# First norms inside the fourth row tile's statistics, K's second half turned earlier, first scores in two query halves: attention with a fused gated FFN on one core

## The chip, the cores and the metric

The kernel runs on one core of one Trainium2 chip. The metric is the device time of one execution in microseconds (us); lower is better. "Same" means within 2% of the kernel before. Times quoted are medians of fast runs unless one run is named; no run of this study fell into the slow state (a single run of a one-core program has no state of its own and is only used as one look).

Engines are named as the profile names them: PE is TensorE's matmul stream, PEld its weight loads, DVE is VectorE, ACT is ScalarE, POOL is GpSimd, SP is the engine that issues most DMAs. Positions in the trace are microseconds from the start of the span.

## The reference

Layer norm, then attention with 32 heads of width 192 over 2048 cached keys, times a gated FFN on the same normed input, with a residual. Cut to what matters:

```python
x: (1, 2048, 640)   k_cache, v_cache: (1, 32, 2048, 192)   wq: (640, 6144)   wo: (6144, 640)   # bf16
xn = _layernorm(x)
q  = (xn @ wq).reshape(B, Sq, H, Dh)
p  = softmax(einsum("bhqd,bhkd->bhqk", q, k_cache) * Dh ** -0.5)
s  = einsum("bhqk,bhkd->bhqd", p, v_cache).reshape(B, Sq, H * Dh) @ wo
g  = _silu((_silu(xn @ w1) * (xn @ w3)) @ w2)
return x + s * g
```

## The kernel before

The kernel walks a stream of steps `(head, query block, key pair)`. Each step does scores on PE, exponentials on ACT, values on PE. Before the stream there is an opening, `head_start`, that has to produce the first normed and transposed inputs, the first head's turned K, and the first projected queries. Query block 0 is built from four row tiles, in two pairs.

```python
def head_start():
    load_x(0, 0, 2); load_x(0, 2, 4)
    load_k0(0, nc.sync)                       # K of head 0, first half
    load_w0()
    turn_over(44)                             # warming matmuls
    ln_stats(0, 0); ln_stats_act(0, 1)
    load_k0(1, nc.scalar)                     # K of head 0, second half
    # ... more loads
    ln_stats(0, 2)
    # ...
    ln_rstd(0, 1)                             # POOL: inverse deviation of the first pair
    ln_stats(0, 3)                            # ends with POOL's work for the second pair
    load_w(1)
    for i in range(4):
        ln_norm(0, i, nc.vector)
    pk0 = ps_o.tile(...)
    ln_turn(0, 0, nc.scalar.copy)             # PE: transpose the first pair
    turn_k0(pk0, 0, range(4))                 # PE: transpose K, first half
    ln_turn(0, 1, nc.vector.tensor_copy)      # PE: transpose the second pair
    turn_k0(pk1, 1, (0, 1))                   # PE: transpose K, second half, first two slices
    swap_halves(0)                            # two DMAs: xnS = xnT with its partition halves exchanged
    # copies of the turned K, loads
    project_first()
    turn_k0(pk1, 1, (2, 3))
    copy_k0(nc.scalar.copy, pk1, 1, 1)
    scores(0)
    shift_first()                             # DVE: queries moved between partition halves
    shift_k0()                                # DVE: the same for K
    scores(1)
    ln_stats(1, 0); ln_stats(1, 1); ln_stats(1, 2)
    ln_norm(1, 0, nc.vector); ln_norm(1, 1, nc.vector)
    ln_turn_dma(1, 0); ln_turn_dma(1, 1)      # transposed by DMA, not by PE
    # ...
```

```python
def swap_halves(g):
    qs = slice(g * 512, (g + 1) * 512)
    nc.sync.dma_start(out=xnS[0:64, :, qs], in_=xnT[64:P, :, qs])
    nc.sync.dma_start(out=xnS[64:P, :, qs], in_=xnT[0:64, :, qs])

def shift_first():
    qAB, qC = q_tiles(0, 0)
    nc.vector.tensor_copy(out=qC[64:P, 0, :], in_=qAB[0][0:64, :])
    nc.vector.tensor_copy(out=qC[0:64, 0, :], in_=qAB[0][64:P, :])

def two_products(W, qs):                      # a projection as pairs of half-height products
    for j in range(2 * DC):
        for r in range(2):
            xs = xnT if j % 2 == r else xnS   # every second operand is the exchanged copy
            nc.tensor.matmul(ps[:, r * 512:(r + 1) * 512], lhsT=W[rows, j, :], rhs=xs[rows, j // 2, qs], ...)
```

Early in the stream, still during head 0's first query block, two projections follow:

```python
if h == 0 and qb == 0 and p == 3:
    project(1, 0)       # two_products: needs xnS of block 0; its result is cast by DVE and ACT
# ... at p == 3 also: ln_turn(1, 1): PE transposes the second pair of block 1 into the buffer that cast has freed
if h == 0 and qb + 1 < NQB and p == (5 if qb == 0 else 4):
    project0(qb + 1)    # qb == 0: needs all of block 1, half of it transposed by ln_turn_dma
```

Of the kernel before, what the change touches and what calls it, by code (L numbers as in the profile page):

```python
# [12 lines left out]
F32 = mybir.dt.float32  # L13
I32 = mybir.dt.int32

P = 128
# [112 lines left out]
def _kernel_impl(  # L129
# [12 lines left out]
    nc = tc.nc  # L142
# [68 lines left out]
    loads = {}  # L211
# [56 lines left out]
    def turn_k0(dst, half, sel):  # L268
        for a in sel:
            for b in range(HP):  # L270
                nc.tensor.transpose(out=dst[:, a, b * P:(b + 1) * P],  # L271
                                    in_=k0["v"][:, half * HP + b, FIRST[a]:FIRST[a] + P], identity=ident_bf[:])
# [32 lines left out]

    lnorm = {}

    def ln_stats(g, i):
        if i == 0:
            lnorm[g] = [lnp.tile([P, 4, n], F32, tag=t, name=t)  # L310
                        for t, n in (("mv", nc.vector.BN_AGGR_DIM), ("ve", 1), ("rstd", 1))]
        mv, ve, rstd = lnorm[g]
        stats = lnp.tile([P, nsub, nc.vector.BN_STATS_DIM], F32, tag="stats", name="stats")
        xr = x_sb[:, 4 * g + i, :].rearrange("p (a f) -> p a f", a=nsub)
        for a in range(nsub):
            nc.vector.bn_stats(out=stats[:, a, :], in_=xr[:, a, :])  # L316
        nc.vector.bn_aggr(out=mv[:, i, :], in_=stats[:])
        if i % 2 == 1:
            nc.vector.tensor_scalar(out=ve[:, i - 1:i + 1, 0], in0=mv[:, i - 1:i + 1, 1], scalar1=eps, scalar2=None,
                                    op0=ALU.add)  # L320
            ln_rstd(g, i)
# [27 lines left out]
    def ln_turn(g, i2, copy):  # L349
        pst = ps_st.tile([P, 2, DC, P], BF16, tag="st2", name="pst")  # L350
        for k in range(2):
            xn = xns.pop((g, 2 * i2 + k))
            for c in range(DC):
                nc.tensor.transpose(out=pst[:, k, c, :], in_=xn[:, c * P:(c + 1) * P], identity=ident_bf[:])  # L354
        q0 = (4 * g + 2 * i2) * P
        copy(out=xnT[:, :, q0:q0 + 2 * P].rearrange("p c (k q) -> p k c q", k=2), in_=pst[:])
# [11 lines left out]
    qtiles = {}  # L368
# [12 lines left out]
    def project_first():  # L381


        W = loads[0]["W"]
        qAB, qC = q_tiles(0, 0)
        for hh in range(2):
            hs = slice(hh * 256, (hh + 1) * 256)
            ps = ps_st.tile([P, 1024], F32, tag="st2", name="ps0")
            for half in range(2):
                for c in range(DC):  # L390
                    nc.tensor.matmul(ps[:, half * 512:half * 512 + 256], lhsT=W[:, half * DC + c, :], rhs=xnT[:, c, hs],  # L391
                                     start=(c == 0), stop=(c == DC - 1))
            i0 = nc.vector.tensor_copy(out=qAB[0][:, hs], in_=ps[:, 0:256])
            i1 = nc.scalar.copy(out=qAB[1][:, hs], in_=ps[:, 512:768])
            tc.declare_no_dep(i1.ins, i0.ins, reason="two banks, two destinations")
        nc.vector.tensor_copy(out=qC[0:64, 1, :], in_=qAB[1][64:P, :])
# [71 lines left out]

    stream = [(h, qb, p) for h in range(H) for qb in range(NQB) for p in range(NPAIR)]

    def emit_scores(h, qb, p):


        KW = loads[h]["KW"]
        (qA, qB), qC = qtiles[h, qb]
        ks = slice(p * P, (p + 1) * P)
        st2 = ps_st.tile([P, 1024], F32, tag="st2", name="st2")
        rounds = [(KW[0:64, 0, ks], qA[0:64, :], KW[64:P, 1, ks], qC[64:P, 0, :]),
                  (KW[0:64, 3, ks], qC[0:64, 0, :], KW[64:P, 4, ks], qA[64:P, :]),
                  (KW[0:64, 1, ks], qC[0:64, 1, :], KW[64:P, 2, ks], qB[64:P, :])]  # L480
        if (h, qb) == (0, 0) and p < 2:
            rounds = rounds[2:]
            nc.tensor.matmul(st2[:, 0:512], lhsT=KW[:, 0, ks], rhs=qA[:], start=True, stop=False)
            nc.tensor.matmul(st2[:, 512:1024], lhsT=KW[:, 4, ks], rhs=qA[:], start=True, stop=False)
        nr = len(rounds)
        for r, (ka, qa, kb, qb2) in enumerate(rounds):
            nc.tensor.matmul(st2[:, 0:512], lhsT=ka, rhs=qa, start=r == 0 and nr == 3, stop=r == nr - 1)  # L487
            nc.tensor.matmul(st2[:, 512:1024], lhsT=kb, rhs=qb2, start=r == 0 and nr == 3, stop=r == nr - 1)  # L488
        pT2 = pp.tile([P, 1024], BF16, tag="pT2", name="pT2")
        parts = 2 if (h, qb, p) == (0, 0, 0) else 1  # L490
        w = 1024 // parts
        for c in range(parts):
            nc.scalar.activation(out=pT2[:, c * w:(c + 1) * w], in_=st2[:, c * w:(c + 1) * w], func=ACT.Exp, scale=att_scale)  # L493
        return pT2
# [75 lines left out]
    def turn_over(k):  # L570
        for i in range(k):
            nc.tensor.matmul(warm, lhsT=ident_bf[:], rhs=ident_bf[:], start=True, stop=True)

    def head_start():

        load_x(0, 0, 2)
        load_x(0, 2, 4)
        load_k0(0, nc.sync)
        load_w0()
        turn_over(44)  # L580
        ln_stats(0, 0)
        ln_stats_act(0, 1)
        load_k0(1, nc.scalar)
        load_x(1, queue=nc.scalar)
        load_v(0, (0,), nc.scalar)
        mv, ve, _ = lnorm[0]
        nc.vector.tensor_scalar(out=ve[:, 0, :], in0=mv[:, 0, 1:2], scalar1=eps, scalar2=None, op0=ALU.add)
        ln_stats(0, 2)
        nc.vector.tensor_scalar(out=ve[:, 1, :], in0=lnorm["ss"][:], scalar1=1.0 / D, scalar2=eps,
                                op0=ALU.mult, op1=ALU.add)  # L590
        ln_rstd(0, 1)
        ln_stats(0, 3)
        load_w(1)
        for i in range(4):
            ln_norm(0, i, nc.vector)
        pk0 = ps_o.tile([P, 4, 512], BF16, tag="ob0", name="pk0")
        ln_turn(0, 0, nc.scalar.copy)
        turn_k0(pk0, 0, range(4))
        ln_turn(0, 1, nc.vector.tensor_copy)
        turn_k0(pk1, 1, (0, 1))  # L600
        swap_halves(0)
        copy_k0(nc.scalar.copy, pk0, 0, 0)
        copy_k0(nc.scalar.copy, pk0, 0, 1)
        copy_k0(nc.vector.tensor_copy, pk1, 1, 0)
        load_v(0, (1,))
        load_x(2)
        project_first()
        turn_k0(pk1, 1, (2, 3))
        copy_k0(nc.scalar.copy, pk1, 1, 1)
        scores(0)  # L610
        shift_first()
        shift_k0()
        scores(1)
        ln_stats(1, 0)
        ln_stats(1, 1)
        ln_stats(1, 2)
        ln_norm(1, 0, nc.vector)
        ln_norm(1, 1, nc.vector)
        ln_turn_dma(1, 0)
        ln_turn_dma(1, 1)  # L620
        for g in range(3, NQB):
            load_x(g)
        ln_stats(1, 3)
# [187 lines left out]
```

## Time and profile before

| | kernel before |
|---|---|
| time, three runs | 1938.18 us (1938.04 to 1938.49) |
| span of the profiled run | 1936.6 us |
| PE busy | 1927.5 us, 99% of the chain |
| first projection starts | 10.34 us |
| first paired round of scores starts | 13.82 us |
| steady stream without waits of PE from | about 40 us |

PE is the chain for practically the whole span. So the only way this change can act on the time is by moving the point at which PE enters its steady stream, and a microsecond won or lost on PE before 40 us should be a microsecond of the total. The lines of the page and of the opening stand in the prediction below. Three more lines of the timeline of the kernel before are needed to follow the first scores to the end of the opening (columns: start, duration, engine, line, operation, output<-inputs, shape, count, and in brackets the idle time before it and what ended it).

```profile
13.82 0.39 PE L487 MATMUL st<-qC,KW 64*128 64x512 bf16 x1
...
19.03 0.38 PE L424 MATMUL ps<-xnT,W 64*128 64x512 bf16 x1
19.27 0.39 PE L424 MATMUL ps<-xnS,W 64*128 64x512 bf16 x2
```

What to see: 13.82 is the first paired round; 19.03 is the first half-product of `project(1, 0)`, which reads xnT; the next pairs come 0.21 to 0.22 apart, but the first one that reads xnS does not come with it, at 19.03, but at 19.27.

### The profile page before, as it was taken

The page shows a single profiled execution, that of the slowest core. Times are in us where ns is not written, and L with a number is a line of the kernel's source. Part 1 is how long each engine was busy: PE and PEld are TensorE (multiplying, and loading weights), DVE is VectorE, ACT ScalarE, POOL GpSimd, SP SyncE. Part 2 cuts the span into 40 slices and gives each one's busy share as a digit, 9 for nine tenths or more (in the row PEclk, how much of TensorE's full clock was granted, in tenths as well). Part 3 has the DMA queues.
Part 4 walks back from the last instruction along what each step waited for, and adds up shares of the span by engine and source line. Part 5 has one row for each costly group of instructions (what it writes and reads, how often), then busy time and mean ns, then how long its engine had stood idle before and what let it go on. Part 6 is the DMA issues. An engine that isn't in the chain of part 4 may idle for free.

```text
span 1936.6 us, 59677 instructions
## 1 busy us (share of the span) xinstructions
PE 1927.5 (100%) x27281; PEld 1316.0 (68%) x27281; DVE 654.4 (34%) x997; ACT 1181.2 (61%) x1279; POOL 282.5 (15%) x501
## 2 busy tenths in 40 slices
PE   9999999999999999999999999999999999999998
PEld 6666666666666666666666666666666666577776
DVE  7333333333333333333333333333333334521111
ACT  6677676767676767776777777677767677210000
POOL 3111111111111111111111111111111110000000
PEclk9999999999999999999999999999999999999999
DMA  8643433324233434363434343434334220937883
GB/s 181 129 101 67 98 68 84 85 60 91 58 90 62 99 64 97 68 162 68 101 66 100 69 101 69 101 64 100 69 71 94 59 68 2 256 71 139 151 153 60
DMA packets 394643, 178.98 MB, mean 92 GB/s; under 512 B 341616, under 2 KB 382832, under 8 KB 394384
## 3 DMA queue, kind: packets, MB, share of 16 engines
q1 hardware_dynamic: 371136, 125.32, 31.7%
q0 software_dynamic: 19472, 45.71, 10.2%
q8 instruction: 215, 3.52, 0.8%
q10 hardware_dynamic: 3776, 4.06, 0.7%
q14 instruction: 44, 0.36, 0.1%
HBM read 52.82 MB, written 27.79 MB: 42 GB/s over the span
## 4 chain that ended last, share of the span: by engine, by line
PE 99%; DVE 1%; DMA 0%; ACT 0%; issue 0%; DVEq 0%; ACTq 0%
PE obank L519 35%; PE st L487 34%; PE ps L424 14%; PE ps_s L111 11%; PE ps_f L731 3%; PE ps_gu L705 1%; PE st L488 1%; PE ps L410 0%; DVE stats L316 0%; DMA x_all<-in_A_x_dram 0%; PE ps L391 0%; PE pst L354 0%; PE pk L271 0%; DVE xn L346 0%; ACT pT L493 0%; DVE osum L529 0%
## 5 line engine op out<-in xcount | busy, mean ns | idle before, releaser
L493 ACT ACTIVATE pT<-st 128x1024 bf16<-128x1024 f32 (+1 forms) x1025 | 1047.1, 1022 | 249.2 <-PE st L488 233.2
L519 PEld LDWEIGHTS <-pT 64*128 64x128 bf16 x16384 | 711.3, 94 | 242.3 <-ACT pT L493 0.6
L519 PE MATMUL obank<-vt,pT 64*128 64x193 bf16 x16384 | 849.7, 243 | 0.0
L487 PE MATMUL st<-qC,KW 64*128 64x512 bf16 x2046 | 605.6, 376 | 0.0
L528 DVE COPY osum<-obank 128x772 f32<-128x772 f32 x128 | 123.1, 962 | 787.1 <-PE obank L519 787.1
L488 PE MATMUL st<-qB,KW 64*128 64x512 bf16 x1024 | 385.0, 376 | 0.0
L487 PE MATMUL st<-qA,KW 64*128 64x512 bf16 x1022 | 384.3, 376 | 0.1
L488 PE MATMUL st<-qC,KW 64*128 64x512 bf16 x1022 | 384.3, 376 | 0.0
L488 PE MATMUL st<-qA,KW 64*128 64x512 bf16 x1022 | 384.3, 376 | 0.0
L487 PEld LDWEIGHTS <-KW 64*128 64x128 bf16 x3068 | 278.5, 94 | 153.7 <-issue 2.1
L424 PE MATMUL ps<-xnT,W 64*128 64x512 bf16 x1280 | 297.2, 376 | 0.0
L424 PE MATMUL ps<-xnS,W 64*128 64x512 bf16 x1280 | 296.0, 376 | 0.0
L488 PEld LDWEIGHTS <-KW 64*128 64x128 bf16 x3068 | 278.5, 94 | 0.5
L377 POOL DMA_DIRECT2D qC<-qA x124 | 65.4, 528 | 1283.1 <-DVE rl_all L535 1268.2
L430 ACT CAST qB<-ps 128x512 bf16<-128x512 f32 x131 | 76.8, 586 | 228.1 <-PE ps L424 222.5
L111 PE MATMUL ps_s<-wo_sb,oT 128*128 128x256 bf16 (+3 forms) x1536 | 208.8, 299 | 0.0
L424 PEld LDWEIGHTS <-W 64*128 64x128 bf16 x2560 | 122.9, 94 | 121.4 <-issue 0.2
L111 PEld LDWEIGHTS <-oT 128*128 128x128 bf16 x1536 | 148.4, 98 | 60.4
L529 DVE TENSOR_TENSOR osum<-osum,obank 128x772 f32<-128x772 f32 x128 | 122.7, 958 | 13.4
L536 DVE TENSOR_TENSOR ostage<-osum,rl_all 128x768 bf16<-128x768 f32 x128 | 122.6, 958 | 6.1 <-DMA o_scr<-ostage 1.8
L465 DVE SCALAR_TENSOR_TENSOR hT<-pt,qB 64x512 bf16<-64x512 bf16 x64 | 43.8, 684 | 197.7 <-ACT pt L464 197.7
L429 DVE CAST qA<-ps 128x512 bf16<-128x512 f32 x131 | 90.6, 692 | 25.4 <-PE ps L410 7.2
(84 smaller groups left out, 623.2 us busy)
## 6 DMA issues: line engine op xcount, KB each, us to landing
o_scr<-ostage SPq DMA_DIRECT2D x16, 1536.0 KB, 10.4
vt<-in_A_v_cache_dram SPq DMA_DIRECT2D x63, 384.0 KB, 5.9
qC<-qA POOLq DMA_DIRECT2D x248, 64.0 KB, 1.9
qC<-qB POOLq DMA_DIRECT2D x124, 64.0 KB, 2.4
wo_sb<-in_A_wo_dram POOLq DMA_DIRECT2D x1, 7680.0 KB, 36.6
W<-in_A_wq_dram POOLq DMA_DIRECT2D x32, 160.0 KB, 3.6
W<-in_B_w_dram POOLq DMA_DIRECT2D x32, 80.0 KB, 3.3
W<-in_A_wq_dram POOLq DMA_DIRECT2D x32, 80.0 KB, 2.9
```

What stands on the lines that cost most here:

```text
L111: nc.tensor.matmul(ps[:, 0:w], lhsT=oT[:, k, :], rhs=wo_sb[:, k, c0:c1], start=(k == 0), stop=(k == OC - 1))
L377: nc.gpsimd.dma_start(out=qC[0:64, half, :], in_=qAB[half][64:P, :])
L424: nc.tensor.matmul(ps[:, r * 512:(r + 1) * 512], lhsT=W[rows, j, :], rhs=xs[rows, j // 2, qs], start=(j == 0), stop=(j == 2 * DC - 1))
L429: a = nc.vector.tensor_copy(out=qAB[0][:], in_=ps[:, 0:512])
L430: b = nc.scalar.copy(out=qAB[1][:], in_=ps[:, 512:1024])
L487: nc.tensor.matmul(st2[:, 0:512], lhsT=ka, rhs=qa, start=r == 0 and nr == 3, stop=r == nr - 1)
L488: nc.tensor.matmul(st2[:, 512:1024], lhsT=kb, rhs=qb2, start=r == 0 and nr == 3, stop=r == nr - 1)
L493: nc.scalar.activation(out=pT2[:, c * w:(c + 1) * w], in_=st2[:, c * w:(c + 1) * w], func=ACT.Exp, scale=att_scale)
L519: nc.tensor.matmul(obanks[r][:, j * 256:j * 256 + DH + 1], lhsT=pT2[r * 64:(r + 1) * 64, t * 512 + j * P:t * 512 + (j + 1) * P], rhs=vt[r ...
L528: nc.vector.tensor_copy(out=osum[:], in_=ov[0])
L529: nc.vector.tensor_tensor(out=osum[:], in0=osum[:], in1=ov[1], op=ALU.add)
L536: nc.vector.tensor_tensor(out=ostage[:, qb * 4:qb * 4 + 4, hg * DH:(hg + 1) * DH], in0=osum[:, :, 0:DH], in1=rl.unsqueeze(2).to_broadcast( ...
```

## The change

Intent: start PE's first transposes earlier by placing the first pair's two norms between the fourth tile's statistics and its aggregate, so that they don't stand behind work of the second pair; let PE turn K's second half while the second pair's norms are still running; and begin the first scores with the first 256 queries, while the second 256 are still being cast. In addition a K copy moves from ACT to DVE, and three warming matmuls go. The diff, cut:

```diff
-    def ln_stats(g, i):
+    def ln_stats(g, i, between=None):
...
             nc.vector.bn_stats(out=stats[:, a, :], in_=xr[:, a, :])
+        if between is not None:
+            between()
         nc.vector.bn_aggr(out=mv[:, i, :], in_=stats[:])
...
+    def half_scores():
+        KW, qA, i = loads[0]["KW"], qtiles[0, 0][0][0], early["half"]
+        early["half"] += 1
+        qs = slice(i * 256, (i + 1) * 256)
+        for b, a in enumerate((0, 4)):
+            nc.tensor.matmul(early["st"][:, b * 512 + i * 256:b * 512 + (i + 1) * 256], lhsT=KW[:, a, 0:P], rhs=qA[:, qs],
+                             start=i == 0, stop=False)
...   (emit_scores skips the two matmuls that half_scores has begun)
-        turn_over(44)
+        turn_over(41)
...
-        ln_stats(0, 3)
+        def first_norms():
+            for i in range(2):
+                ln_norm(0, i, nc.vector)
+
+        ln_stats(0, 3, first_norms)
         load_w(1)
-        for i in range(4):
+        for i in range(2, 4):
             ln_norm(0, i, nc.vector)
...
         turn_k0(pk0, 0, range(4))
+        turn_k0(pk1, 1, (0, 1))
         ln_turn(0, 1, nc.vector.tensor_copy)
-        turn_k0(pk1, 1, (0, 1))
...
         project_first()
+        first_scores()
+        half_scores()
         turn_k0(pk1, 1, (2, 3))
-        copy_k0(nc.scalar.copy, pk1, 1, 1)
+        copy_k0(nc.vector.tensor_copy, pk1, 1, 1)
+        half_scores()
         scores(0)
```

More of the change, by code (lines that the diff above doesn't have):

```diff
@@ L469, in _kernel_impl, with first_scores @@
     stream = [(h, qb, p) for h in range(H) for qb in range(NQB) for p in range(NPAIR)]
+    early = {}
+    def first_scores():
+        early["st"] = ps_st.tile([P, 1024], F32, tag="st2", name="st2")
+        early["half"] = 0
+    def half_scores():
[5 more added lines that the diff above has]
+                             start=i == 0, stop=False)
     def emit_scores(h, qb, p):
@@ L476, in emit_scores @@
         ks = slice(p * P, (p + 1) * P)
-        st2 = ps_st.tile([P, 1024], F32, tag="st2", name="st2")
+        st2 = early.pop("st", None)
+        begun = st2 is not None
+        if not begun:
+            st2 = ps_st.tile([P, 1024], F32, tag="st2", name="st2")
         rounds = [(KW[0:64, 0, ks], qA[0:64, :], KW[64:P, 1, ks], qC[64:P, 0, :]),
@@ L482, in emit_scores @@
             rounds = rounds[2:]
-            nc.tensor.matmul(st2[:, 0:512], lhsT=KW[:, 0, ks], rhs=qA[:], start=True, stop=False)
-            nc.tensor.matmul(st2[:, 512:1024], lhsT=KW[:, 4, ks], rhs=qA[:], start=True, stop=False)
+            if not begun:
+                nc.tensor.matmul(st2[:, 0:512], lhsT=KW[:, 0, ks], rhs=qA[:], start=True, stop=False)
+                nc.tensor.matmul(st2[:, 512:1024], lhsT=KW[:, 4, ks], rhs=qA[:], start=True, stop=False)
         nr = len(rounds)
```

## The prediction

> **What bounds the kernel now.** I read the page first, for the engine that sets the end and for the chain that ended last.
>
> ```profile
> PE 1927.5 (100%) x27281; PEld 1316.0 (68%) x27281; DVE 654.4 (34%) x997; ACT 1181.2 (61%) x1279; POOL 282.5 (15%) x501
> ...
> PE 99%; DVE 1%; DMA 0%; ACT 0%; issue 0%; DVEq 0%; ACTq 0%
> ```
>
> TensorE is busy for the whole span and is the chain for 99% of it. The diff touches only the opening, about the first 14 us, so the steady part (a repeating 1.3 us of scores and values on PE) is worth the same before and after. The question is how late PE enters that steady part. So the second view is the timeline of the opening.
>
> ```profile
> 4.64 0.39 ACTq L265 DMA_DIRECT2D kn<-in_A_k_cache_dram  x1
> ...
> 6.06 0.87 DVE L316 BATCH_NORM_STATS2 stats<-x_all 128x6 f32<-128x320 bf16 x2
> 6.25 0.72 POOL L327 TENSOR_TENSOR rstd<-ve,mhalf 128x2 f32<-128x2 f32 x1 [1.83 <-DVE ve L589]
> 6.97 0.21 DVE L317 BATCH_NORM_AGGREGATE mv<-stats 128x2 f32<-128x12 f32 x1
> 7.21 0.17 DVE L319 TENSOR_SCALAR ve<-mv 128x2 f32<-128x2 f32 x1
> 7.29 0.80 DVE L346 TENSOR_SCALAR xn<-x_all,mv,rstd 128x640 bf16<-128x640 bf16 x2
> 7.46 0.82 POOL L327 TENSOR_TENSOR rstd<-ve,mhalf 128x2 f32<-128x2 f32 x1 [0.50 <-DVE ve L319]
> ...
> 8.32 0.91 DVE L346 TENSOR_SCALAR xn<-x_all,mv,rstd 128x640 bf16<-128x640 bf16 x2 [0.23 <-POOL rstd L327]
> ...
> 8.44 1.06 PE L271 MATMUL pk<-ident_bf,kn 128*128 128x128 bf16 x16
> ...
> 9.33 0.72 PE L354 MATMUL pst<-ident_bf,xn 128*128 128x128 bf16 x10
> ...
> 9.89 0.61 PE L271 MATMUL pk<-ident_bf,kn 128*128 128x128 bf16 x8
> ...
> 10.34 2.35 PE L391 MATMUL ps<-xnT,W 128*128 128x256 bf16 x20
> ```
>
> What to see: the first pair's inverse deviation is ready on POOL at 6.97 (6.25 + 0.72), but DVE spends 6.97 to 7.38 on the fourth row tile's aggregate and its addition before the first norm at 7.29. PE goes 16 K turns, 10 turns of the second pair, 8 K turns, projection, without a gap from 8.44. Then I looked at when the loads land, by tile: first kn, then xnS.
>
> ```profile
> DMA to landing us min/median/max: 5.1/5.4/5.7
> ```
>
> ```profile
> L365 SPq DMA_DIRECT2D xnS<-xnT x1: 613/613/613, 11.8 to 11.8; - x1
> ...
> DMA to landing us min/median/max: 6.7/7.1/7.5
> ```
>
> K's halves were issued at 1.7 and 4.6; the second lands at 4.6 + 5.1 = 9.7 (4.6 + 5.7 = 10.3 is excluded, since PE turns that half from 9.89). So K's second half has only some 0.2 us of slack today. xnS lands at 11.8 + 7.5 = 19.3, and the first product that reads it starts at 19.27: a second gate. Last, the timeline from 14 to 30 us, for DVE:
>
> ```profile
> 14.47 0.89 DVE L316 BATCH_NORM_STATS2 stats<-x_all 128x6 f32<-128x320 bf16 x2
> ...
> 25.02 2.32 PE L410 MATMUL ps<-xnT,W 128*128 128x512 bf16 x10
> ...
> 27.38 0.69 DVE L429 CAST qA<-ps 128x512 bf16<-128x512 f32 x1
> ...
> 28.63 0.28 DVE L415 COPY qC<-qB 64x512 bf16<-64x512 bf16 x1
> ...
> 29.03 0.38 PE L487 MATMUL st<-qC,KW 64*128 64x512 bf16 x1
> ```
>
> Between 14.47 and 28.9 DVE has four idle moments only (0.81 for POOL's next pair, 0.27 and 0.25 for PE, none after 23.60); the last scores round at 29.03 starts 0.12 after the copy that feeds it ends (28.63 + 0.28). DVE is nearly the bound of this stage, though its share over the span is 34%.
>
> **What the Trainium skill says.** "TensorE: Matmul & The Clock Gate", Step-by-step: PE may pull a weight load ahead, but the matmuls stay in program order. So a turn that waits for its load holds up all that is behind it; in this trace PE indeed runs in program order throughout. "DMA: Bandwidth & Descriptors", Why a DMA increments its semaphore by 16 and not by 1: only the full count means that all data landed, so the slowest of the 16 engines decides; the 5.1 us of the kn load, for 384 KB at 316 GB/s, fit a late last part. The same page, Queues, rings and completion order: each DMA engine round-robins between queue rows with work; the windows view gives a DMA share of 1.01 from 2.77 to 8 us, 1.13 from 8 to 14 and 1.19 from 14 to 22, so transfers are throughput-bound, and a transfer issued later may land at the same time. "TensorE: Matmul & The Clock Gate", What's actually happening: the clock falls back after an idle window of about 3.4 us; the gap before the first turns is 0.81 us and the granted clock is 1.00 in every window, so three warming turns fewer (44 to 41, 3 x 0.1 us) cost nothing as long as that gap remains under a microsecond.
>
> **The change, part by part.**
>
> First norms. POOL's result at 6.97, plus the 0.04 that the second pair shows (8.28 to 8.32), gives the first norm at 7.01 rather than 7.29: 0.28 earlier. First turns follow 0.50 after it (7.29 to 7.79), so at 7.51; the first K half's 16 turns at 8.16 and done starting at 9.05 (8.44 and 9.33, less 0.28). But aggregate and addition now wait for both norms: aggregate at 7.80, addition 8.04 to 8.21, POOL 8.29 to 9.11, second pair's norms 9.15 to 10.05 rather than 8.32 to 9.23: 0.82 later.
>
> K's second half ahead. PE asks for it at 9.05; it lands at about 9.7. A new wait of 0.7, which PE in program order cannot step around. Its 8 turns (0.056 each, from 16 in 0.89) then run 9.80 to 10.25, the second pair's 10 turns 10.25 to 10.81, and the projection starts at 10.81 against 10.34: 0.47 later. Had the half landed by 9.05, the second pair's norms (10.05) would still hold the last five turns until 10.10 and the projection until 10.38: no gain either.
>
> First scores in halves. The projection takes 2.2 us as before and ends at about 13.1. The second query half's cast is done 0.46 later (13.62), while PE runs the first half's two matmuls and the 8 K turns; the second half's two matmuls at 13.68, the paired round behind them at about 14.10 against 13.82. From projection to that round is 3.29 rather than 3.48: this part gives 0.19 back. Net, PE and the exponentials are 0.28 late.
>
> The K copy from ACT (1.01 us) to DVE (0.68, as DVE's other copy of that shape at 10.83). ACT was not the limit there any more than PE. DVE gets the copy in front of its three shifts: copy 13.97 to 14.65, shifts and K shift to 15.6, next statistics at 15.65 rather than 14.47: 1.18 late.
>
> Downstream. xnS is issued after the second pair's transposed copy, which ends at 11.83 instead of 10.91; with the DMA engines saturated I expect it to land near 19.3 still, and PE arrives at 19.31: even. DVE's 1.18 is cut by the waits it makes unnecessary: 0.27 before the cast at 21.62 (now 22.5), and some 0.25 before the transposed copy at 23.60 (now about 24.26, 0.66 late). PE's turns of that stage wait for that cast's buffer, 0.42; of this about 0.15 to 0.2 is hidden, since the projection at 25.02 waits today for a transfer. So that projection starts about 0.3 later. DVE at 0.66 late holds the round of 29.03 until 29.6; the wait PE has at 34.99 (0.36, for DVE) takes part of that back. After 40 us PE has no more waits, so what is left stays to the end.
>
> Sum: -0.28 (norms) + 0.75 (wait for K, and the norms behind) - 0.19 (halves) = +0.28 at the first scores, and +0.3 to +0.45 after 40 us. I take +0.35: 1938.18 + 0.35 is 1938.5.
>
> **Rivals.** One: the chain is as the change intends, K's second half lands early enough in the execution timed, and the first scores start 0.2 to 0.3 early. For it: the half-split removes a real wait, and landing times may move from run to run. Against it: the second pair's norms, and xnS at 19.3, a gate that an earlier PE only meets sooner. This would give 1937.8 to 1938.2. Two: every gain or loss before 19 us is swallowed by that gate and by the one at 25.02, since both are set by saturated DMA engines: 1938.1 to 1938.3. Against it: DVE's lateness reaches beyond both. Three: xnS, and the two transposing transfers that the projection at 25.02 needs (now issued about 1.2 later), are bound by their issue after all; then that projection starts up to 1 us later: 1938.9 to 1939.3. Against it: the DMA share over 1 in these windows.
>
> **Range and chances.** The three runs of before spread by 0.45. The mechanisms span -0.4 to +1.1. So 1937.8 to 1939.2, with 1938.5 in it. 2% are 39 us; the whole opening is 14, so a change within 2% is as good as certain.
>
> **What would show it.** In the profile after: first norm at about 7.0 and first turns at 7.5 (else the POOL step is wrong). PE's second-half K turns at 9.7 to 9.8 with a wait for that load in front (if they start near 9.1, the main step is wrong, and so is the sign). Second pair's norms at 9.15. Projection at 10.8. First paired round at 14.1. Statistics of the second block on DVE at 15.6. Product with xnS still near 19.3. Projection now at 25.02 near 25.3. If the last two come at the old times or earlier, the time is that of before or less, and the sum downstream is what failed.

## The result, and the profile after

| | before | changed |
|---|---|---|
| median of six runs | 1938.38 us | 1938.57 us |
| range | 1938.04 to 1940.34 | 1938.16 to 1939.06 |
| ratio | | 0.9999 (95%: 0.9986 to 1.0012) |
| span of the profiled run | 1936.6 | 1936.6 |

A ratio here is the mean time of the changed kernel's runs over the mean of the other kernel's runs of the same rounds, so it is not quite the ratio of the medians. The two kernels take the same time. The mean of before is pulled up by two runs (1939.49 and 1940.34), and the medians stand the other way round, by 0.19 us; neither difference is clear of the spread. From here on, differences of tenths are read in the traces, where a start is given to 0.01 us, with the reservation that each kernel has one trace (the changed one two), and that the landing of loads differs between executions.

The page of the changed kernel, engine totals and chain:

```profile
PE 1927.3 (100%) x27272; PEld 1317.2 (68%) x27280; DVE 654.8 (34%) x998; ACT 1179.1 (61%) x1278; POOL 282.3 (15%) x501
...
PE 99%; DVE 0%; DMA 0%; issue 0%; ACT 0%; POOL 0%
```

It is the same page as before to within 0.3%; what the change does must be looked for in the opening, which is all that the diff touches. The timeline of the changed kernel's opening:

```profile
6.88 0.80 DVE L348 TENSOR_SCALAR xn<-x_all,mv,rstd 128x640 bf16<-128x640 bf16 x2
7.59 0.20 DVE L319 BATCH_NORM_AGGREGATE mv<-stats 128x2 f32<-128x12 f32 x1
...
8.08 0.70 POOL L329 TENSOR_TENSOR rstd<-ve,mhalf 128x2 f32<-128x2 f32 x1 [1.24 <-DVE ve L321]
8.81 0.90 DVE L348 TENSOR_SCALAR xn<-x_all,mv,rstd 128x640 bf16<-128x640 bf16 x2 [0.81 <-POOL rstd L329]
9.58 0.62 PE L271 MATMUL pk<-ident_bf,kn 128*128 128x128 bf16 x8 [0.49 <-DMA kn<-in_A_k_cache_dram]
...
10.60 2.35 PE L393 MATMUL ps<-xnT,W 128*128 128x256 bf16 x20
...
13.65 0.69 DVE L277 COPY KW<-pk 128x1024 bf16<-128x1024 bf16 x1
13.78 0.38 PE L509 MATMUL st<-qC,KW 64*128 64x512 bf16 x1
...
15.34 0.89 DVE L316 BATCH_NORM_STATS2 stats<-x_all 128x6 f32<-128x320 bf16 x2
...
18.99 0.59 PE L426 MATMUL ps<-xnS,W 64*128 64x512 bf16 x2
...
22.14 0.68 DVE L431 CAST qA<-ps 128x512 bf16<-128x512 f32 x1
22.88 0.73 PE L356 MATMUL pst<-ident_bf,xn 128*128 128x128 bf16 x10 [0.26 <-DVE qA L431]
24.96 2.33 PE L412 MATMUL ps<-xnT,W 128*128 128x512 bf16 x9
```

Read against the kernel before:

- The first norm starts at 6.88 instead of 7.29. The first statistics started at 3.65 instead of 3.77, because x landed 0.12 earlier in this execution, so 0.29 of the 0.41 belongs to the change.
- The price: POOL's step for the second pair starts at 8.08 instead of 7.46, and that pair's norms at 8.81 instead of 8.32.
- K's second half is now asked for at 9.09 and PE waits 0.49 for it. The projection starts at 10.60 instead of 10.34.
- From projection to first paired round PE takes 3.18 instead of 3.48: the two query halves. So that round starts at 13.78 instead of 13.82. In front, the change is 0.04 ahead. This part of the gain repeats: the stretch is 3.18 or 3.19 in all eleven traces that have the halves, 3.48 in all three that don't.
- DVE, with the K copy added at 13.65, starts the second block's statistics at 15.34 instead of 14.47.
- The projection `project0(1)` starts at 24.96 instead of 25.02, and the one of the next query block at 39.09 instead of 39.04. The 0.11 between is a gate of the same kind: the exchange of block 1 landed at 31.54 (30.98 before), and the next product with it started at 31.59, 0.38 after its xnT neighbour, where before the two start together at 31.23. The projection that this product belongs to ends 0.36 behind (its last product at 33.53 against 33.17), and all but 0.05 is made up again by 39 us. At the end the spans differ by 0.05 (1936.58 and 1936.63).

### A sum for the way from 14 to 25 us

Between the first paired round and `project0(1)` PE has a fixed amount of work. Two runs below (e10 and e12) show it without any wait: 5.22 from the round to the first product with xnS (13.84 to 19.06, 13.89 to 19.11) and 5.65 from there to `project0(1)` (19.06 to 24.71, 19.11 to 24.76). For every kernel that keeps this order of PE's work (e5 and e8 change it), then,

start of `project0(1)` = first paired round + 5.22 + lost before xnS + 5.65 + lost after it.

| kernel | round | lost before xnS | lost after | project0(1) |
|---|---|---|---|---|
| before | 13.82 | 0.23 | 0.10 | 25.02 |
| changed | 13.78 | 0.00 | 0.32 | 24.96 |

Before loses 0.23 at xnS (landed 19.23) and 0.10 at the tiles that DMA transposes (the second landed at 24.89). The changed kernel, in the execution that was profiled, got xnS earlier (18.60, though its last exchange was issued at 12.46 rather than 11.75), and lost 0.26 of its 0.32 instead to DVE's late cast of qA. So two theories stand:

- **Theory A, transfers.** xnS and the DMA-transposed tiles land when the DMA engines have worked through what is queued, nearly independently of when PE is ready. What the front gains is lost there again.
- **Theory B, DVE.** The K copy and the reordered norms make DVE late, and this lateness, handed on through the cast, is what cancels the gain.

(The expectations below call B theory 1; A is theory 2 there, and in e2 the rival.)

### The profile page after: what moved, and what is told of

It reads as the page before. It is cut to its first block, busy times and chain, and to the rows that moved or that the text cites. A ratio compares the mean times of both kernels' runs of the same rounds, so it can differ in the third digit from the quotient of the medians.

```text
span 1936.6 us, 59666 instructions
## 1 busy us (share of the span) xinstructions
PE 1927.3 (100%) x27272; PEld 1317.2 (68%) x27280; DVE 654.8 (34%) x998; ACT 1179.1 (61%) x1278; POOL 282.3 (15%) x501
## 4 chain that ended last, share of the span: by engine, by line
PE 99%; DVE 0%; DMA 0%; issue 0%; ACT 0%; POOL 0%
PE obank L541 35%; PE st L509 33%; PE ps L426 14%; PE ps_s L111 11%; PE ps_f L761 3%; PE ps_gu L735 1%; PE st L510 1%; PE ps L412 0%; DMA kn<-in_A_k_cache_dram 0%; DVE stats L316 0%; DMA x_all<-in_A_x_dram 0%; PE ps L393 0%; DVE xn L348 0%; PE pst L356 0%; DVE mv L319 0%
## 5 line engine op out<-in xcount | busy, mean ns | idle before, releaser
L111 PE MATMUL ps_s<-wo_sb,oT 128*128 128x384 bf16 (+3 forms) x1535 | 208.8, 299 | 0.1
L431 DVE CAST qA<-ps 128x512 bf16<-128x512 f32 x131 | 90.6, 691 | 25.2 <-PE ps L412 7.3
```

Of the source, the lines that this page charges most:

```text
L111: nc.tensor.matmul(ps[:, 0:w], lhsT=oT[:, k, :], rhs=wo_sb[:, k, c0:c1], start=(k == 0), stop=(k == OC - 1))
L431: a = nc.vector.tensor_copy(out=qAB[0][:], in_=ps[:, 0:512])
```

## The experiments

Three groups of four kernels; each group ran on one chip together with runs of the kernel before, but a different chip each time, and the kernel before has one trace only, taken apart from the three groups. All twelve gave correct results. "Round", "lost" and "project0(1)" are the columns of the sum above.

### e1_again: the changed kernel once more

No edit.

> The changed kernel unchanged, to see how far one profile of it agrees with another. Both theories expect the same marks as in its first profile, within 0.2 us: first turns 7.4, K's second half 9.6 after a wait for its load, first projection 10.6, first paired round 13.8, second block's statistics on DVE 15.3, product with xnS 19.0, projection of the second query block 25.0. Time 1938.2 to 1939.1, and no verdict against the kernel before.

Measured: 1938.30 us (1938.13 to 1939.59, five runs) against 1938.66 (1937.82 to 1940.63, nine runs) of before, ratio 0.9997 (0.9983 to 1.0011). The timeline of this second trace of the same code:

```profile
9.62 0.86 PE L356 MATMUL pst<-ident_bf,xn 128*128 128x128 bf16 x10
...
15.06 0.89 DVE L316 BATCH_NORM_STATS2 stats<-x_all 128x6 f32<-128x320 bf16 x2
...
18.70 0.38 PE L426 MATMUL ps<-xnT,W 64*128 64x512 bf16 x1
19.29 0.39 PE L426 MATMUL ps<-xnS,W 64*128 64x512 bf16 x2 [0.21 <-DMA xnS<-xnT]
...
25.13 2.32 PE L412 MATMUL ps<-xnT,W 128*128 128x512 bf16 x10
```

The view of the tile kn says why the front looks different:

```profile
DMA to landing us min/median/max: 3.7/3.9/4.1
```

K's second half landed at 8.46 here and at 9.53 in the first trace. So PE had no wait for it and the round started at 13.49, 0.33 ahead of before: 0.03 of it at the projection (10.31), 0.30 from the two query halves. Of the expected marks all but the last missed by more than the 0.2 allowed. The gain in front was of no use: xnS landed at 19.24, the product with it started at 19.29, 0.59 after the xnT product that it normally stands beside (0.58 by the sum). The sum is 13.49 + 5.22 + 0.58 + 5.65 + 0.19 = 25.13, later than before. Theory A describes this execution: DVE was 0.59 late at 15.06 and PE waited for it nowhere.

### e2_pool_shifts: DVE relieved, nothing else

```diff
-        nc.vector.tensor_copy(out=KW[0:64, 3, :], in_=KW[64:P, 0, :])
+        nc.gpsimd.tensor_copy(out=KW[0:64, 3, :], in_=KW[64:P, 0, :])
...   (the two copies of shift_first likewise; shift_k0 is called ahead of shift_first)
```

> The changed kernel with its three partition shifts (two of q, one of K) on GpSimd instead of DVE: 0.29 + 0.29 + 0.42 us less on DVE before the second block's statistics. Theory 1 (DVE's lateness takes the gain of the opening back): statistics start at about 14.4 instead of 15.34, the cast at 22.14 moves to about 21.4, the transposes on PE lose their 0.26 us wait and start at 22.55, the second block's projection at 24.7 instead of 24.96, the span is about 0.3 shorter (1936.3). Rival (the transfers set the pace at 25 us: transposed tiles landing 24.4 to 24.9): statistics earlier too, but that projection remains at 24.9 to 25.0 and the span at 1936.6.

Measured: 1938.38 us, ratio 0.9998 (0.9984 to 1.0011). Timeline:

```profile
14.42 0.89 DVE L316 BATCH_NORM_STATS2 stats<-x_all 128x6 f32<-128x320 bf16 x2
...
19.47 0.39 PE L426 MATMUL ps<-xnS,W 64*128 64x512 bf16 x2
...
21.82 0.69 DVE L431 CAST qA<-ps 128x512 bf16<-128x512 f32 x1 [0.52 <-PE ps L426]
...
25.19 2.32 PE L412 MATMUL ps<-xnT,W 128*128 128x512 bf16 x10
```

DVE's lateness is gone: its statistics start at 14.42, as early as before, and at 21.82 it is DVE that waits for PE, by 0.52. And `project0(1)` starts at 25.19, no earlier than with the lateness (24.96 and 25.13). PE lost 0.41 before xnS (landed 19.43) and 0.07 after. In this execution, where xnS landed late, removing B's cause alone gains nothing; 25.19 is later than both theories had it.

### e3_k_order: K's second half back behind the second pair

```diff
-        turn_k0(pk1, 1, (0, 1))
         ln_turn(0, 1, nc.vector.tensor_copy)
+        turn_k0(pk1, 1, (0, 1))
```

> The changed kernel with K's second half turned behind the second pair again (that part undone). If the wait for K's load (0.49 us) is what costs: the second pair's turns start at about 9.35, its copy on DVE at 10.3 instead of 10.80, the projection at 10.5 instead of 10.60. So only 0.1 us at the projection, since the second pair's norms end at 9.7 now and hold the turns. Theory 1: the rest unchanged, second block's statistics at 15.2 to 15.3, its projection at 24.9 to 25.0. Rival (the K wait alone ate the gain): projection at 10.2, everything 0.4 earlier.

Measured: one look, 1938.44 us. PE waited 0.23 for the second pair's norms instead of for K; the projection started at 10.57, the round at 13.75. K landed at 9.42, so this compares with the first trace of the change (K at 9.53, wait 0.49, projection at 10.60): which of the two comes first on PE made a difference of 0.03 when K lands late. When it lands early (e1), the change's order gains: 10.31. Downstream xnS landed at 19.53, 0.60 was lost there and nothing after: 25.22.

### e4_copy_act: the K copy back on ACT

```diff
-        copy_k0(nc.vector.tensor_copy, pk1, 1, 1)
+        copy_k0(nc.scalar.copy, pk1, 1, 1)
```

> The changed kernel with the last K copy on ACT as before (that part undone): DVE is relieved of 0.68 us, ACT takes 1.01 us between the last cast and the first exponential. Theory 1: statistics at about 14.65, first exponential at 14.7 instead of 14.22, PE's transposes without a wait for the cast, the second block's projection at 25.2 to 25.4: the front loses what the back gains. Rival (DVE's lateness is free, only the first exponential counts): the projection 0.45 later, 25.4 or more, and the same shift still there at 39 us.

Measured: one look, 1939.00 us, span 1937.2. The copy takes 1.01 us on ACT at 13.61, and stands in front of the first exponentials there: the first products with the values come at 15.18, 0.33 later than the round allows (from the round at 13.75, 1.10 is usual). xnS cost a further 0.38 and the tiles 0.12: `project0(1)` at 25.45, the latest of the first group. DVE's statistics were 0.64 earlier than in the first trace of the change (14.70), and that brought nothing here. In this one trace the copy was better off on DVE.

### e5_one_pair_later: more time for xnS

```diff
-        if h == 0 and qb == 0 and p == 3:
+        if h == 0 and qb == 0 and p == 4:
             project(1, 0)
...   (the second transposes of block 1 and their exchange also one pair later)
```

> The changed kernel with the next head's first projection (the one that reads xnS) and the second pair of transposes of block two done one pair of score tiles later: the gate at xnS is taken out of PE's way. In four of five profiles PE waited at 19.0 to 19.7 for xnS's landing plus 0.05. Theory 2 (two transfer gates, xnS and then the DMA-transposed tiles, set the pace): PE passes 19.3 with no wait, the product with xnS comes at about 20.2 with xnS landed 0.6 to 1.2 before, but the projection of the second query block stays within 0.15 us behind the landing of the transposed tiles (24.4 to 25.1), so 24.6 to 25.2, and the span is 1936.4 to 1936.7. Theory 1 (DVE's lateness sets it): DVE's cast moves to after PE's product at 22.4 to 23.1 and the projection comes at 25.3 or later. If neither holds, that projection comes at 24.3 to 24.6 and the span is 0.4 to 0.6 shorter.

Measured: one look, 1940.04 us, span 1938.3. The xnS product started at 20.13 beside its xnT neighbour, without a wait (xnS landed at 19.20). But the statistics of block 2 stayed where they were and now stood in front of the cast on DVE: PE waited 1.40 for that cast before the transposes at 25.16 and 0.92 for the copy behind them. My own edit made the delay (the cast, which theory 1 put at 22.4 to 23.1, came at 24.43); the run only shows that the wait at xnS goes when the consumer is moved. It doesn't decide between A and B. (Its front was also slowed by PE's clock; see the part on the warming turns below.)

### e6_swap_split: the exchange in two parts, the first issued earlier

```diff
+    def swap_part(q0, q1):
+        nc.sync.dma_start(out=xnS[0:64, :, q0:q1], in_=xnT[64:P, :, q0:q1])
+        nc.sync.dma_start(out=xnS[64:P, :, q0:q1], in_=xnT[0:64, :, q0:q1])
...
         ln_turn(0, 0, nc.scalar.copy)
+        swap_part(0, 256)
...
-        swap_halves(0)
+        swap_part(256, 512)
```

> The changed kernel with the exchange of halves (xnS) issued in two parts, the first pair's columns already after its copy at 9.5, the second pair's where it was. If xnS's landing is bound by its issue, the late half is now only 320 KB and it lands about 1 us earlier, at 18.2 to 18.5, and PE does not wait there. If it is bound by what the DMA engines have to move in all (theory 2), the runs of 512 B are no faster, it lands at 19.0 or later and the product with it is still at 19.1 to 19.8. The projection of the second query block then follows the transposed tiles in both, 24.9 to 25.2.

Measured: one look, 1938.17 us, span 1936.3. Timeline:

```profile
18.78 0.56 PE L430 MATMUL ps<-xnS,W 64*128 64x512 bf16 x2
...
22.65 0.73 PE L356 MATMUL pst<-ident_bf,xn 128*128 128x128 bf16 x10 [0.23 <-DVE qA L435]
...
24.73 2.33 PE L416 MATMUL ps<-xnT,W 128*128 128x512 bf16 x10
```

The first part was issued at 9.86 and the last at 12.05; the last landed at 18.74. The round had started at 13.55, and the product with xnS at 18.78: only 0.01 lost. `project0(1)` came at 24.73, earlier than both theories had said, and the landing lies between their two ranges (18.2 to 18.5, 19.0 or later), so it doesn't say why the split helps. What remains is B's: 0.23 of waiting for DVE's cast, 0.30 lost after the product. So the two theories are not rivals but two gates one behind the other. Where xnS lands late, PE is held there, and DVE catches up meanwhile; where it lands early, PE runs into DVE's lateness.

### e7_copy_twice: DVE made later on purpose

```diff
         copy_k0(nc.vector.tensor_copy, pk1, 1, 1)
+        copy_k0(nc.vector.tensor_copy, pk1, 1, 1)
```

> The changed kernel with the last K copy done twice on DVE (same data, result right): DVE another 0.65 us late. Statistics of block two at 16.0 instead of 15.06 to 15.34. Theory 1 (DVE is the bound from 14 to 29 us): all of it arrives on PE: the cast for the next head at 22.6 to 22.8, PE's transposes wait for it until 23.4 or later, the projection of the second query block at 25.6, the span at 1937.2. Theory 2 (transfers set the pace, DVE has 0.3 to 0.5 us of slack behind them): the transposes at 23.4, the projection at 25.2 to 25.4, the span 1936.8 to 1937.0.

Measured: one look, 1939.23 us, span 1937.5. DVE's second-block statistics start at 16.27, 0.93 later than in the first trace of the change, and the transposes read:

```profile
23.80 0.73 PE L356 MATMUL pst<-ident_bf,xn 128*128 128x128 bf16 x10 [0.80 <-DVE qA L431]
```

`project0(1)` is at 25.88, 0.75 to 0.92 later than in the two traces of the change. (0.20 of the difference to the first trace is a later round, 13.98, since K landed at 9.7.) Of an extra copy of 0.71 on DVE, 0.54 comes out as a longer wait of PE (0.80 against 0.26). That is beyond what either theory expected (25.2 to 25.6). So B is a real cost, and behind this change DVE had no more than a few tenths of slack left in this trace.

### e8_fewer_bytes: the next head's weights loaded later

The edits of e2 and e5, and:

```diff
         ln_stats(0, 3, first_norms)
-        load_w(1)
...
         shift_k0()
         shift_first()
+        load_w(1)
```

> As the one-pair-later kernel, with the three shifts on GpSimd and the next head's 480 KB of weights issued behind them, at about 15.0 instead of 8.7: those bytes leave the stretch before xnS. If the landing of xnS hangs on the bytes before it (theory 2), it lands 1 us or more earlier than 18.6 to 19.6, at 17.3 to 18.4; if on its own issue, at 18.6 to 19.6 as before. The weights then land at 20.5 to 22 and may hold the next head's projection at about that time. The transposed tiles, behind all bytes in both cases, land at 24.4 to 25.1 and the second query block's projection follows within 0.15 us, unless the weights' wait is longer; span 1936.4 to 1937.

(The weights are 320 KB, not 480: W is 128 x 1280 in bf16.)

Measured: one look, 1943.45 us, span 1941.7, the slowest of all. The 320 KB of weights, issued behind POOL's shifts at 14.3 to 15.8, landed at 20.3 to 23.3, and `project(1, 0)` itself stood waiting for them:

```profile
23.39 0.39 PE L426 MATMUL ps<-xnS,W 64*128 64x512 bf16 x2 [2.69 <-DMA W<-in_A_wq_dram]
```

The weights put too late are my mistake, and the time says nothing on the theories. But one thing of it does: xnS landed at 16.52, against 19.20 in e5, though issued only 0.34 earlier (last exchange at 11.95 and 12.29). Taking 320 KB out of the traffic ahead of it brought it 2.7 us forward, while xnS landed between 18.60 and 19.64 in every trace with these loads and the exchange in one part. That is A's mechanism by itself: here the landing of xnS followed the bytes that compete with it, not its own issue.

The second loss in this run is PE's clock. The windows view of this kernel (window; its length; then busy time with counts of PE, PEld, DVE, ACT, POOL; granted clock; DMA share; GB/s):

```profile
23.30:26.80 3.50, 3.41 (x19) 1.56 (x21) 1.94 (x7) 0.00 (x0) 0.69 (x1) 0.58 0.63 207
```

After the pause the clock was granted at 0.58 and the product's pairs came up to 0.43 apart instead of 0.21 to 0.22: from its first xnS pair to its last product it took 3.38 (23.39 to 26.77) instead of the 1.94 of before (19.27 to 21.21).

### e9_split_pool: both gates moved

The edits of e6 and e2 together.

> The changed kernel with both gates moved: the exchange of halves issued in two parts (as in the split run, where xnS no longer held PE, transposed tiles landed at 21.8 and the second query block's projection came at 24.73), and the three shifts on GpSimd, which brings DVE's statistics to about 14.3. If DVE is the one bound left behind the split (theory 1 then holds once theory 2's gate is gone): the cast for the next head follows PE at 21.2 to 21.4, the transposes start at 22.3 to 22.5 without a wait, that projection at 24.3 to 24.5, the span 1935.9 to 1936.1, 0.5 to 0.7 under the kernel before. If a third gate stands there: 24.7 and 1936.3 again. The time cannot show it clear of noise: runs of one kernel spread by 0.9 to 2.8 us.

(One figure in this expectation is misread: a landing of 21.8 that I took for the transposed tiles' was that of x's third block. In e6 those tiles landed at 24.46.)

Measured: 1938.01 us (1937.64 to 1938.83, five runs) against 1938.28 (1937.90 to 1942.53, nine runs) of before, ratio 0.9995 (0.9982 to 1.0009); span 1936.24. Round 13.57, lost 0.14 before xnS (landed 18.89), 0.09 after (tiles landed 24.54), `project0(1)` at 24.67. That is 0.35 ahead of before, and the best of the kernels with the change in them, but not the 24.3 to 24.5 expected if no other gate stood there: the gates were moved, not gone.

### e10_before_split: the kernel before with the split exchange alone

The edit of e6, made in the kernel before.

> The kernel before with the exchange issued in two parts, nothing else: what that alone is worth, and so what the change is worth where xnS is no gate. DVE is not late here (statistics 14.47, cast right after PE's product), so if the transfer gates were all that held it, PE passes xnS at 19.05 instead of 19.27 and the second query block's projection comes 0.4 earlier, at 24.6 or so, with the span at 1936.1 to 1936.2: as early as the changed kernel with the same split (24.73, 1936.3) or earlier, which would say that the change gains nothing even there, because DVE's lateness takes it. If the change has a gain of its own there, this run is behind that one: 24.9 or later, 1936.5.

Measured: one look, 1937.92 us, span 1936.15. Timeline:

```profile
19.06 0.59 PE L428 MATMUL ps<-xnS,W 64*128 64x512 bf16 x2
...
24.71 2.33 PE L414 MATMUL ps<-xnT,W 128*128 128x512 bf16 x10
```

No loss at either gate (xnS landed 18.73, tiles 24.39): 13.84 + 5.22 + 5.65 = 24.71. The split alone moves `project0(1)` 0.31 forward in the kernel before, as much as e9 has over before less 0.04. So what e9 has over the kernel before comes from the split, but for 0.04 (one trace each).

### e11_split_pool_k: K's second half asked for earlier

e9, with `load_k0(1)` issued on SP right behind `load_k0(0)`:

```diff
         load_k0(0, nc.sync)
+        load_k0(1, nc.sync)
...
-        load_k0(1, nc.scalar)
```

> As the split-and-shifts kernel, with K's second half issued on the sync queue right behind the first instead of from ACT at 4.6: the wait for K (0 to 0.49 us from profile to profile, with K landing between 8.5 and 9.7) is taken away. If that wait costs: K's turns start at 8.9 to 9.1 straight behind the first half's, the projection at 10.2 to 10.4 (the second pair's norms hold it then), the first paired round 13.3 to 13.5, the second query block's projection 0 to 0.2 before that of the split-and-shifts kernel. If the earlier K load only delays the load of q's weights and the rest of x, the projection comes no earlier and the span is the same or up to 0.3 longer.

Measured: 1938.95 us (1938.14 to 1939.56, five runs), ratio 0.9999 (0.9986 to 1.0013); span 1936.8. PE did not wait for K, and the round started at 13.44, the earliest of the kernels in the table below. But:

```profile
19.40 0.39 PE L430 MATMUL ps<-xnS,W 64*128 64x512 bf16 x2 [0.37 <-DMA xnS<-xnT]
```

xnS landed at 19.35 instead of 18.89, split or not, and the tiles too came late: 0.74 lost before, 0.26 after, `project0(1)` at 25.31. So this was worse than both branches of the expectation. That the bytes of K pulled forward pushed back those behind them fits (the last part of head 0's weights landed at 10.05 instead of 8.38), but one trace does not show it to be the only reason. The earliest front in the table gave one of its later ends.

### e12_before_split_pool: e9 without the change

The edits of e6 and e2, made in the kernel before. Against e9 it tells what the change is worth when both gates have been moved.

> The kernel before with both the split exchange and the shifts on GpSimd: what remains of the change's own gain where neither gate stands. DVE's statistics at 13.5 or so; DVE has 1 us to spare. If the change's opening is worth 0.2 to 0.3 us by itself (first paired round 13.5 to 13.6 against 13.82), this kernel's second query block's projection is 0.2 to 0.3 behind that of the changed kernel with the same two edits, at about 24.6 to 24.7, span 1936.2. If not, both are equal within 0.1.

Measured: 1938.15 us (1937.94 to 1939.05, five runs), ratio 0.9997 (0.9983 to 1.0011); span 1936.17. Round 13.89, nothing lost, `project0(1)` at 24.76. In e9 the round is 0.32 earlier, and 24.67 is 0.09 earlier; at the next query block's projection 0.10 earlier (38.69 and 38.79). Of the 0.32, then, 0.23 was lost at the two gates, which hold e9 and not e12. Yet the span of e9 is 0.07 longer (1936.24): from that projection to the end it took 1897.55 us, e12 1897.38. So even this tenth can't be told from noise. What the front would be worth with no gate behind it, no run shows.

### All of it in one table

| kernel | round | xnS landed | lost before xnS | lost after | project0(1) | span |
|---|---|---|---|---|---|---|
| before | 13.82 | 19.23 | 0.23 | 0.10 | 25.02 | 1936.6 |
| changed | 13.78 | 18.60 | 0.00 | 0.32 | 24.96 | 1936.6 |
| e1, changed again | 13.49 | 19.24 | 0.58 | 0.19 | 25.13 | 1936.7 |
| e2, DVE relieved | 13.84 | 19.43 | 0.41 | 0.07 | 25.19 | 1936.6 |
| e3, K's order back | 13.75 | 19.53 | 0.60 | 0.00 | 25.22 | 1936.7 |
| e4, copy on ACT | 13.75 | 19.64 | 0.71 | 0.12 | 25.45 | 1937.2 |
| e6, split exchange | 13.55 | 18.74 | 0.01 | 0.30 | 24.73 | 1936.3 |
| e7, copy twice | 13.98 | 19.16 | 0.17 | 0.86 | 25.88 | 1937.5 |
| e9, split, relieved | 13.57 | 18.89 | 0.14 | 0.09 | 24.67 | 1936.2 |
| e11, and K earlier | 13.44 | 19.35 | 0.74 | 0.26 | 25.31 | 1936.8 |
| e10, before, split | 13.84 | 18.73 | 0.00 | 0.00 | 24.71 | 1936.2 |
| e12, before, split, relieved | 13.89 | 18.76 | 0.00 | 0.00 | 24.76 | 1936.2 |

Read down the rows without the split: the round ranges over half a microsecond, from 13.49 to 13.98, and xnS lands between 19.16 and 19.64 in all but one. Since xnS does not land earlier for an earlier round, the round's gain comes back as "lost before xnS" (0.33 of e4's 0.71 is not xnS but the copy on ACT). With the split, xnS lands at 18.73 to 18.89, except in e11, and `project0(1)` is at 24.67 to 24.76 whether the round starts at 13.55 or at 13.89.

## Why the prediction was right, and where it wasn't

The time on record, 1938.5, is 0.07 from the median measured, and the verdict is as predicted. The verdict was safe: 2% is 39 us, and the change acts on the first 14. The closeness of the time is luck. It was the base of 1938.18 plus 0.35; in the six runs the median of before became 1938.38, the medians differ by 0.19, the means by 0.19 the other way round, and the traces have the change 0.05 and 0.10 behind at 39 us. So the steps deserve a harder look.

**First norms: right.** 7.01 predicted, 6.88 measured, of which 0.12 is an earlier x. First turns at 7.51 and 7.38.

**Second pair's norms: right in kind, too late in size.** 9.15 predicted, 8.81 measured. The 0.34 are three parts: 0.13 from the earlier first norm; 0.08 because the aggregate starts 0.71 after the norms, not 0.79 (I had added whole durations; in the trace the aggregate starts at 7.59, before the norms end at 7.68); and 0.12 because POOL took 0.70, not the 0.82 that I copied from one instance.

**Three warming turns fewer: no cost in the two traces of the change, but a cost in others.** The windows view gives a granted clock of 1.00 from 2.77 us on, and the prediction took that at its word. But the clock record in these traces begins only when the full clock is granted, and the view shows 1.00 where there is no record too. Until that moment the matmuls came 107 ns apart, from then on 56 ns. The full clock came at 6.14 in the kernel before, at 7.13 and 7.42 in the two traces of the change, whose first turns follow at 7.38 and 7.63. In e5, e6 and e7 it came at 8.60, 8.24 and 7.74, after the first turns (7.40, 7.51, 7.45), which came 107 ns apart until then. In e5:

```profile
7.40 1.25 PE L356 MATMUL pst<-ident_bf,xn 128*128 128x128 bf16 x10
```

These ten take 0.81 in the first trace of the change. The projection of e5 started at 10.42, that of e8, with K as early and the second norms at the same time within 0.02, at 10.09. So the gap before the first turns (0.81 us before, 0.09 in the changed kernel) was the wrong thing to watch; the margin from the full clock to the first turn was the right one. It was 0.59 to 1.65 in the three traces with 44 warming matmuls, and from +1.13 down to -1.20 in the eleven with 41. How much of that is the three matmuls, how much the earlier turns and how much the spread of executions, no run separates.

**The wait for K: right that it comes, wrong as a constant.** 0.7 predicted, 0.49 in the first trace, none in the second, 0.15 in e9, 0.58 in e7. Issued at the same place, K's second half landed anywhere between 8.46 and 9.7 in the traces. I had taken one execution's landing for a property of the kernel. With K early the prediction saw no gain at the projection (10.38); it came at 10.31 in e1 and 10.09 in e8, against 10.34, since the second pair's norms came earlier than I had them.

**First paired round at 14.10, +0.28: this is the term that was mis-sized, and its sign was wrong.** Measured 13.78 and 13.49, so -0.04 and -0.33. In the first trace 0.21 of the difference is the smaller K wait and the rest of the front (projection at 10.60, not 10.81), and 0.11 is the two query halves, which were worth 0.30 rather than 0.19. As the prediction's first rival said, the round comes early when K does (by 0.21 to 0.55 in e1, e5, e6, e8, e9 and e11), and 0.30 of that are the two halves.

**DVE 1.18 late at the second block: right in kind, too large.** 0.87 and 0.59 measured, since the round, and with it the copy, came earlier.

**xnS near 19.3 still: right in one trace, by luck in the other.** 18.99 and 19.29 for the product; but in the first trace xnS had landed at 18.60, and 18.99 is when PE got there. That a later issue would not mean a later landing held: issued up to 0.7 later, it landed 0.6 earlier in one trace and at the same time in the other.

**`project0(1)` at 25.3, and +0.35 left at the end: too late.** 24.96 and 25.13; at 39 us the change was 0.05 and 0.10 behind. In particular the round that I expected to slip from 29.03 to 29.6 did not: the copy that feeds it started at 28.66, against 28.63 before. The prediction added DVE's lateness to the waits for transfers. The runs show that they lie behind one another and absorb each other: while PE is held by xnS, DVE catches up (e1, e3), and DVE's lateness shows where xnS is early (first trace, e6) or where DVE is made later still (e7). (A slip of reading besides: the prediction speaks of four idle moments of DVE up to 28.9; the trace has the three that it lists.)

**The rivals.** The second one, that the gates at 19 us and 25 us swallow whatever happens in front, is what most runs bear out: e1 shows it in the changed kernel, e11 in the extreme, and e9 against e12 with the gates moved. What was put against it, that DVE reaches beyond both gates, is true in one of the two traces and worth 0.26 there. The third rival, an issue-bound exchange costing up to 1 us, didn't come.

What stays open: whether the changed kernel is really 0.05 to 0.1 us slower, as its two traces have it, or equal. The before's own medians went from 1938.18 to 1938.66 between groups of runs, so the times can't tell. Nor was it shown that the split exchange is faster in time: the profiled spans with it (1936.15 to 1936.31, e11 apart) lie below those of the other traces (from 1936.6), but the intervals of e9 and e12 include 1, and runs of the kernel before on the chip of e9 had spans of 1936.1 and 1936.2 too. By the traces it is the best version, and it needs the split only, not the change. Two parts of the change, the first norms and the fewer warming matmuls, were never undone by themselves. And what makes one and the same load land a microsecond earlier or later from execution to execution was not looked into.

## What to carry to other kernels

Before reordering the front of a pipeline, list the later points at which the critical engine meets a transfer, and ask whether these are set by issue or by throughput: here a gain of 0.33 us in front of a landing that the traffic sets was handed back there in full (e1). Write the path as a sum of fixed work and losses at named gates, as in the table above; it shows in one line where a gain went. And take the landing of a load under traffic from several executions, never from one.

## What the Trainium skill lacked or had wrong

- "DMA: Bandwidth & Descriptors", Latency and other measured facts: it gives a fixed cost of about 2 us and a longer HBM access at high load, but no spread of landing under traffic. Here the last part of the same 384 KB load landed 3.7 us after its issue in one trace and 5.0 in another of the same kernel (8.46 and 9.53), enough to make or remove a wait of 0.49 on PE. Taking 320 KB of other loads out of its way brought the last transfer of an exchange within the core (two of 320 KB) from 19.20 to 16.52.
- "GPSIMD Engine Reference", Engine selection: single-input work is called roughly line-rate there. The three copies between partition halves took 0.71, 0.61 (64x512 bf16) and 1.03 us (64x1024 bf16) on POOL and 0.29, 0.29 and 0.42 us on DVE, so 2.1 to 2.5 times as long. PE waited for none of them in e2 and e9. (Spans on POOL are rough in this profile.)
- "TensorE: Matmul & The Clock Gate", What's actually happening: it ties the fall of the clock to an idle window of about 3.4 us. In e8 waits of 0.36 and 2.69 us with one matmul of 0.39 between them, 3.44 us in all, were followed by a granted clock of 0.58 in the next 3.5 us. How much activity in a window keeps the clock up is not said there.
